# Fillers for TensorE's waits, GpSimd copies of V, and more PSUM banks for the u transposes, in the first two batches of a fused attention and mixer kernel

## The chip, the cores and the metric

The kernel runs on one core of one Trainium2 chip. The metric is the device time in microseconds of one execution. A core has TensorE (PE in the profile; PEld is its weight load), VectorE (DVE), ScalarE (ACT), GpSimd (POOL) and SyncE (SP, which here only issues DMAs). Matmul results go to PSUM, which has eight banks of 2 KB per partition; the other engines run their own instruction streams in order and wait for each other by semaphores.

## The reference

Eight batches of sliding-window causal attention (8 heads, 576 positions, head size 64, window 64), followed by a mixer: a low-rank mix over positions and a two-layer MLP over the 512 channels, each with a residual.

```python
scores = scale * np.matmul(q, k.transpose(0, 1, 3, 2))
scores = np.where((rel >= 0) & (rel < 64), scores, -1e9)      # rel = query pos - key pos
attn = softmax(scores); o = np.matmul(attn, v)
x = o.transpose(0, 2, 1, 3).reshape(B, S, H * D)              # 8 x 576 x 512
h = x.transpose(0, 2, 1) @ U @ V                              # U 576x32, V 32x576
u = x + h.transpose(0, 2, 1)
ch = np.maximum(u @ w_ch1, 0.0) @ w_ch2                       # 512 -> 2048 -> 512
return u + ch
```

## The kernel before

All 4608 tokens (8 x 576) are cut into 36 tiles of 128 and nine chunks of 512. The work of a batch comes in pieces:

- T: `TK(j)` and `TQ(j)` transpose K and Q of a pair of heads on PE (line 245: for the first four batches twelve small transposes). ACT copies the K result into `kt` (line 263), DVE the Q result into `qt` (line 268).
- S: `SC(j)` computes the scores of a pair of heads (line 275), ACT takes the exponential into `pts` (line 290), DVE multiplies with the 0/1 `maskA` (line 291). `SC8` does the last block of all heads.
- PV: `PV(t)` multiplies with V for one tile of 128 positions (line 321); DVE takes reciprocals of the sums and scales into `x` (lines 330, 331). V is held twice: `vA` as it is loaded, and `vB` shifted by 64 positions. The shift is made by `shift_v` (lines 135 and 136 in two large copies, lines 140 and 141 in seven copies of 64 x 512).
- U and V: five matmuls with `ub` (U in bf16, cast from `uf`), an ACT copy into `hh`, then the matmuls with `vrep` (the mixer's V, four times below each other) on line 360. Batches 0 and 1 (`alone`) add x by a matmul with the identity (line 368), and DVE and ACT copy the sums into the tiles `un` (line 383).
- UT: `UT(t)` transposes a tile of u on PE (line 398) and copies it into `uTc`, the input of the MLP (line 402).

The MLP of a chunk, `mlp(c)`, has 16 pieces `ch1` (four matmuls each, `psA`, line 424, then ReLU into `c1`) and 16 pieces `ch2` (four matmuls each, `psU`, line 446; after every fourth, DVE adds u and SP issues the output). The order is written out by hand. Batch 0's attention runs first and alone. Then, for chunk c, the pieces of batch c+1 (and T of batch c+2 from batch 3 on) are put behind the MLP's 32 pieces by tables of slots: `PLACE_1` for batch 1, `PLACE_2` for batch 2, `PLACE` for the rest. Slot 32 is behind the last MLP piece. Each engine runs its instructions in the order in which they are written.

PSUM: `ps_mm` has three banks (MLP results, and three of four transpose groups of batch 0), `ps_big` two buffers of two banks (scores, PV, U, V), `ps_tp` one bank (the other transposes). Batch 0's `shift_v` is done by ACT, between the scores and PV:

```python
a["S"][HP]()
for _ in load_kq(2, False):
    pass
shift_v(0, nc.scalar.copy, range(NFULL))
for f in a["PV"]:
    f()
```

Most loads are issued by POOL and cast to bf16 on the way: K and Q of batch 0, its V, `vrep`, the halves of `w1b` and `w2b`, then K, Q and V of batch 1, in this order. POOL also makes the identity and `maskA` (lines 163 to 181).

Of the kernel before, what the change touches and what calls it, by code (L numbers as in the profile page):

```python
# [12 lines left out]
BF16 = mybir.dt.bfloat16  # L13
FP32 = mybir.dt.float32
# [3 lines left out]
def kernel(  # L18
# [39 lines left out]
    const = ctx.enter_context(tc.tile_pool(name="const", bufs=1))  # L58
# [6 lines left out]
    ps_mm = ctx.enter_context(tc.tile_pool(name="ps_mm", bufs=3, space=bass.MemoryType.PSUM))  # L65
    ps_big = ctx.enter_context(tc.tile_pool(name="ps_big", bufs=2, space=bass.MemoryType.PSUM))
    ps_tp = ctx.enter_context(tc.tile_pool(name="ps_tp", bufs=1, space=bass.MemoryType.PSUM))

    ctx.enter_context(tc.manual_schedule())

# [6 lines left out]
    uf = [const.tile([P, NT, R], FP32, name=f"uf{i}") for i in range(2)]  # L77
    ub = [const.tile([P, NT, R], BF16, name=f"ub{i}") for i in range(2)]
    vrep = const.tile([P, W + S + W], BF16, name="vrep")
    xs = [const.tile([P, NT, H, D], BF16, name=f"xs{i}") for i in range(2)]  # L80
    vA = [const.tile([P, NFULL, H, VW], BF16, name=f"vA{i}") for i in range(2)]
    vB = [const.tile([P, NFULL, H, VW], BF16, name=f"vB{i}") for i in range(2)]
# [49 lines left out]
    def shift_v(b, copy, tiles=None):  # L132
        va, vb = vA[b % 2], vB[b % 2]
        if tiles is None:
            copy(out=vb[0:W, :, :, 0:D], in_=va[W:P, :, :, 0:D])
            copy(out=vb[W:P, 0 : NFULL - 1, :, 0:D], in_=va[0:W, 1:NFULL, :, 0:D])
            return
        for t in tiles:
            if t > 0:
                copy(out=vb[W:P, t - 1, :, 0:D], in_=va[0:W, t, :, 0:D])  # L140
            copy(out=vb[0:W, t, :, 0:D], in_=va[W:P, t, :, 0:D])
# [59 lines left out]
        out=uf[1][:, 1:NT, :], in_=moe_U[W:S, :].rearrange("(c p) r -> p c r", p=P)  # L201
    )
    for g in range(4):
        nc.gpsimd.dma_start(out=vrep[g * R : (g + 1) * R, W : W + S], in_=moe_V[:, :])
    w1v = moe_w_ch1.rearrange("(c p) n -> p c n", p=P)
    for lo, hi in ((0, 1024), (1024, 2048)):
        nc.gpsimd.dma_start(out=w1b[:, :, lo:hi], in_=w1v[:, :, lo:hi])
    w2v = moe_w_ch2.rearrange("(i p) m -> p i m", p=P)
    for lo, hi in ((0, 8), (8, 16)):
        nc.gpsimd.dma_start(out=w2b[:, lo:hi, :], in_=w2v[:, lo:hi, :])  # L210
# [7 lines left out]
    def uT_of(c):  # L218
        if c not in uT_tiles:
            uT_tiles[c] = uT_pool.tile([P, NDC, CH], BF16, name="uTc")  # L220
        return uT_tiles[c]


    def attention(b, spare=False, alone=False):
# [9 lines left out]

        def tr(src, j):
            if grouped:
                if spare and turn[0] % 4 != 0:
                    tpb = ps_mm.tile([P, 2 * CH], BF16, name="tpm", tag="mm")
                    tp = tpb[:, 0:S].rearrange("d (c p) -> d c p", c=GR)
                else:  # L240
                    tp = ps_tp.tile([P, GR, GP], BF16, name="tpg", tag="tp")
                turn[0] += 1
                for c in range(GR):
                    for g in range(2):
                        nc.tensor.transpose(  # L245
                            tp[g * D : (g + 1) * D, c, :], src[:, 2 * j + g, c, :], ident[0:GP, 0:GP]
                        )
# [145 lines left out]
        def UT(t):  # L393
            def f():
                g = g0 + t
                tp = ps_tp.tile([P, NDC, P], BF16, name="tpu", tag="tp")
                for dc in range(NDC):
                    nc.tensor.transpose(  # L398
                        tp[:, dc, :], u_tiles[g][:, dc * P : (dc + 1) * P], ident[:]
                    )  # L400
                col = (g % TPC) * P
                nc.scalar.copy(out=uT_of(g // TPC)[:, :, col : col + P], in_=tp[:])  # L402
            return f

        pcs["T"] = [f for j in range(HP) for f in (TK(j), TQ(j))]
# [10 lines left out]
    def mlp(c):  # L416
        uTc = uT_of(c)
        c1 = [None] * NFC

        def ch1(i):  # L420
            def f():
                ps = ps_mm.tile([P, CH], FP32, name="psA", tag="mm")
                for dc in range(NDC):
                    nc.tensor.matmul(  # L424
                        ps[:],
                        w1b[:, dc, i * P : (i + 1) * P],
                        uTc[:, dc, :],
                        start=(dc == 0),
                        stop=(dc == NDC - 1),
                    )  # L430
                c1[i] = c1_pool.tile([P, CH], BF16, name=f"c1_{i}")
                if i in DVE_RELU:
                    nc.vector.tensor_relu(out=c1[i][:], in_=ps[:])
                else:
                    nc.scalar.activation(out=c1[i][:], in_=ps[:], func=ACT.Relu)
            return f

        acc = {}

        def ch2(t, quarter):  # L440
            def f():
                g = c * TPC + t
                if quarter == 0:
                    acc[t] = ps_mm.tile([P, DM], FP32, name="psU", tag="mm")
                for i in range(4 * quarter, 4 * quarter + 4):
                    nc.tensor.matmul(  # L446
                        acc[t][:],
                        c1[i][:, t * P : (t + 1) * P],
                        w2b[:, i, :],
                        start=(i == 0),  # L450
                        stop=(i == NFC - 1),
                    )
# [17 lines left out]
        "UT": [24, 25, 26, 27, 28],  # L470
    }
    PLACE_1 = {
        "T": [22, 23, 24, 25, 26, 27, 28, 28],
        "S": [24, 26, 28, 29, 29],
        "PV": [30, 31, 32, 32, 32],
        "U": [32],
        "V": [32, 32, 32],
        "UT": [32, 32, 32, 32, 32],
# [3 lines left out]
    PLACE_2["S"] = [3, 5, 7, 9, 10]  # L482


    att = {0: attention(0, spare=True, alone=True)}
    a = att[0]
    for j in range(HP):
        a["T"][2 * j]()
        a["T"][2 * j + 1]()
        if j > 0:  # L490
            a["S"][j - 1]()
    a["S"][HP - 1]()
    a["S"][HP]()
    for _ in load_kq(2, False):
        pass
    shift_v(0, nc.scalar.copy, range(NFULL))
    for f in a["PV"]:
        f()
    for i in range(2):
        nc.vector.tensor_copy(out=ub[i][:], in_=uf[i][:])  # L500
    for part in ("U", "V", "UT"):
        for f in a[part]:
            f()
    load_v(2)


    for c in range(NCH):
        slots = [[] for _ in range(NSLOT + 1)]

        def place(b, parts, where):  # L510
            if b not in att:
                att[b] = attention(b, alone=(b == 1))
            for part in parts:
                for f, s in zip(att[b][part], where[part]):
                    slots[s].append(f)

# [51 lines left out]
```

## Time and profile before

| | |
|---|---|
| median of 3 runs | 378.45 us (378.31 to 379.71) |
| the profiled execution | 379.35 us, its span 377.3 us |
| PE busy | 343.0 us, 91% of the span |
| DVE, ACT, POOL busy | 177.5, 131.1, 108.6 us |
| granted TensorE clock, mean | 0.973 |
| 0 to 30 us: PE busy | 16.4 us |
| 65 to 95 us: PE busy | 20.6 us |

The span is from the first to the last instruction of the profiled execution. The granted clock is the share of TensorE's full clock that the chip allowed, 1.00 being full speed; a row of a busy-time view gives it for its stretch. In a row of the instructions in order of time stand the start and the duration in us, the engine and the kernel's line, the operation with what it writes and reads, and in brackets how long the engine had been idle before it and what released it. The end of a matmul is modelled, so the pace of a stream of matmuls is read from the distance of their starts.

### The profile page before, as it was taken

The numbers are of one execution on the slowest core, as the hardware profiler recorded it, in microseconds if no ns is written. First come the engines' busy times: TensorE is split into PE (matmuls) and PEld (weight loads), VectorE is DVE, ScalarE is ACT, GpSimd is POOL, SyncE is SP. The second block draws the span as 40 slices with busy tenths as digits, with TensorE's granted clock in tenths as the row PEclk, the third lists the DMA queues.
The fourth block names the chain that finished last, engine by engine and source line by source line (L and its number), as shares of the span: only waits on it lengthen the run. The fifth ranks groups of instructions, "written<-read, shape, count | busy, mean of one in ns | idle before, by whom it ended". The sixth has DMA issues, their size and how long they took to land.

```text
span 377.3 us, 7086 instructions
## 1 busy us (share of the span) xinstructions
PE 343.0 (91%) x3030; PEld 170.1 (45%) x3082; DVE 177.5 (47%) x313; ACT 131.1 (35%) x200; POOL 108.6 (29%) x125
## 2 busy tenths in 40 slices
PE   3566999666999999999999999999999999999996
PEld 2433444323544544554455445544554445444442
DVE  4551323550665636554655465546455653322421
ACT  2734213314552345234523452344235403300300
POOL 8761184088008700484038304300000000000000
PEclk9997999886999999999999999999999999999999
DMA  7999999299009910999099809100010002002002
GB/s 95 139 209 200 190 171 197 55 112 105 3 2 118 129 57 0 92 99 112 2 93 108 102 3 90 57 30 0 30 57 28 2 30 84 0 30 83 0 30 84
DMA packets 91135, 28.54 MB, mean 76 GB/s; under 512 B 77152, under 2 KB 85472, under 8 KB 91104
## 3 DMA queue, kind: packets, MB, share of 16 engines
q0 software_dynamic: 84704, 18.50, 56.6%
q1 hardware_dynamic: 6400, 9.59, 7.4%
q8 instruction: 24, 0.39, 0.4%
q14 instruction: 7, 0.06, 0.0%
HBM read 37.14 MB, written 9.44 MB: 123 GB/s over the span
## 4 chain that ended last, share of the span: by engine, by line
PE 84%; DVE 5%; ACT 5%; issue 2%; POOL 2%; DMA 1%; ACTq 0%; DVEq 0%; POOLq 0%
PE psA L424 35%; PE psU L446 31%; PE xr L321 3%; PE tpn L251 3%; PE psv L360 3%; PE sc L275 3%; PE tpu L398 3%; PE tpg L245 2%; ACT pts L290 1%; PE pshh L345 1%; ACT uTc L402 1%; DMA qg<-in_q_dram 1%; DVE xs_97 L331 1%; DVE osb L455 1%; PE psv L368 1%
## 5 line engine op out<-in xcount | busy, mean ns | idle before, releaser
L424 PE MATMUL psA<-uTc,w1b 128*128 128x512 bf16 x556 | 135.0, 388 | 2.0 <-ACT uTc L402 0.7
L424 PEld LDWEIGHTS <-w1b 128*128 128x128 bf16 x576 | 53.9, 99 | 63.3 <-issue 5.2
L455 DVE TENSOR_TENSOR osb<-psU,un 128x512 f32<-128x512 f32 x36 | 24.8, 690 | 59.5 <-PE psU L446 56.5
L291 DVE TENSOR_TENSOR pts<-pts,maskA 128x1024 bf16<-128x1024 bf16 x32 | 23.0, 719 | 36.3 <-ACT pts L290 36.3
L290 ACT ACTIVATE pts<-sc 128x1024 bf16<-128x1024 f32 x32 | 32.7, 1022 | 14.7 <-PE sc L275 14.7
L402 ACT COPY uTc<-tpu 128x512 bf16<-128x512 bf16 x36 | 21.1, 586 | 32.3 <-PE tpu L398 32.3
L123 POOL DMA_DIRECT2D vA_99<-in_v_dram x16 | 14.1, 884 | 54.7 <-PE xr L321 47.4
L123 POOL DMA_DIRECT2D vA_98<-in_v_dram x16 | 14.1, 883 | 38.9 <-PE xr L321 33.5
L321 PEld LDWEIGHTS <-pts 128*64 128x64 bf16 x576 | 14.7, 115 | 18.7 <-issue 11.7
L398 PE MATMUL tpu<-ident,un 128*128 128x128 bf16 x144 | 14.7, 228 | 5.6 <-ACT uTc L402 5.6
L398 PEld LDWEIGHTS <-un 128*128 128x128 bf16 x144 | 11.3, 101 | 13.4 <-issue 6.5
L360 PE MATMUL psv<-hh,vrep 128*128 128x512 bf16 x38 | 14.6, 428 | 2.0 <-ACT hh L353 1.3
L245 PE MATMUL tpg<-ident,kg 96*64 96x96 bf16 x168 | 7.0, 224 | 8.0 <-DMA kg<-in_k_dram 5.2
L331 DVE TENSOR_TENSOR xs_97<-xr,rcp 128x512 bf16<-128x512 f32 (+1 forms) x20 | 13.8, 692 | 0.7
L331 DVE TENSOR_TENSOR xs_96<-xr,rcp 128x512 bf16<-128x512 f32 (+1 forms) x20 | 13.8, 690 | 0.7
L245 PEld LDWEIGHTS <-kg 96*64 96x64 bf16 x192 | 6.6, 125 | 13.8 <-issue 6.7
L330 DVE RECIPROCAL rcp<-xr 128x8 f32<-128x8 f32 (+1 forms) x40 | 8.2, 204 | 9.7 <-PE xr L321 9.6
L385 DVE TENSOR_TENSOR un<-psv,xs_97 128x512 bf16<-128x512 f32 (+1 forms) x15 | 9.8, 687 | 5.2 <-PE psv L360 5.2
L385 DVE TENSOR_TENSOR un<-psv,xs_96 128x512 bf16<-128x512 f32 (+1 forms) x15 | 9.5, 683 | 3.4 <-PE psv L360 3.4
L353 ACT CAST hh<-pshh 128x512 bf16<-128x512 f32 x8 | 4.7, 589 | 16.7 <-PE pshh L345 16.7
L321 PE MATMUL xr<-vA_99,pts 128*64 128x65 bf16 x160 | 8.9, 197 | 1.6 <-DVE xs_97 L331 1.4
L114 POOL DMA_DIRECT2D kn_103<-in_k_dram x10 | 8.7, 872 | 4.9 <-PE tpn L251 4.9
(571 smaller groups left out, 609.6 us busy)
## 6 DMA issues: line engine op xcount, KB each, us to landing
out_dram<-osb SPq DMA_DIRECT2D x36, 256.0 KB, 2.0
vA_98<-in_v_dram POOLq DMA_DIRECT2D x16, 128.0 KB, 5.1
w1b<-in_moe_w_ch_dram POOLq DMA_DIRECT2D x2, 1024.0 KB, 10.2
w2b<-in_moe_w_ch_dram POOLq DMA_DIRECT2D x2, 1024.0 KB, 17.7
vA_99<-in_v_dram POOLq DMA_DIRECT2D x16, 128.0 KB, 4.6
kg<-in_k_dram POOLq DMA_DIRECT2D x3, 576.0 KB, 13.1
qg<-in_q_dram POOLq DMA_DIRECT2D x3, 576.0 KB, 14.2
kn_102<-in_k_dram POOLq DMA_DIRECT2D x8, 128.0 KB, 4.4
```

The costliest lines, as they stand in the source:

```text
L123: nc.gpsimd.dma_start(out=va[:, t, :, 0:D], in_=v[b, :, t * P : (t + 1) * P, :].rearrange("h p d -> p h d"),)
L245: nc.tensor.transpose(tp[g * D : (g + 1) * D, c, :], src[:, 2 * j + g, c, :], ident[0:GP, 0:GP])
L290: nc.scalar.activation(out=dst, in_=sc[:], func=ACT.Exp, scale=scale)
L291: nc.vector.tensor_tensor(out=dst, in0=dst, in1=maskA.rearrange("p g n w -> p g (n w)"), op=ALU.mult)
L321: nc.tensor.matmul(xr[r0 : r0 + W, h // 4, (h % 4) * VW : (h % 4 + 1) * VW], pts[:, h // 2, h % 2, blk, :], rhs, start=True, stop=True,)
L331: nc.vector.tensor_tensor(out=x[lo:hi, t, :, :].rearrange("p (a h) d -> p a h d", a=2), in0=xv[:, :, :, 0:D], in1=rcp[lo:hi].to_broadcast( ...
L360: nc.tensor.matmul(ps[:, n, :], vrep[:, off : off + P], hh["sb"][:], start=True, stop=not alone,)
L398: nc.tensor.transpose(tp[:, dc, :], u_tiles[g][:, dc * P : (dc + 1) * P], ident[:])
L402: nc.scalar.copy(out=uT_of(g // TPC)[:, :, col : col + P], in_=tp[:])
L424: nc.tensor.matmul(ps[:], w1b[:, dc, i * P : (i + 1) * P], uTc[:, dc, :], start=(dc == 0), stop=(dc == NDC - 1),)
L446: nc.tensor.matmul(acc[t][:], c1[i][:, t * P : (t + 1) * P], w2b[:, i, :], start=(i == 0), stop=(i == NFC - 1),)
L455: nc.vector.tensor_tensor(out=osb[:], in0=acc[t][:], in1=u_tiles[g][:], op=ALU.add)
```

## The change

Five things are changed, all in what runs before and during the MLP of the first chunk:

1. Batch 0's `shift_v` is done by POOL, behind the issues of `w1b` and ahead of those of `w2b`.
2. `vrep` is no longer loaded with a cast by POOL. SP loads it in float32 into the new tile `vf`, and DVE casts it, behind the first mask of batch 0; the casts of `uf` to `ub` move to the same place from behind PV.
3. In batches 0 and 1, `UT(t)` takes a bank of the `mm` pool for t not divisible by 4, and DVE makes the copy for even t.
4. `turn_over(n)` issues n matmuls of the identity with 256 columns of `maskA` into a bank that nobody reads. It is called behind transposes, PV, U, V and UT of batch 0, and behind the pieces of batch 1 in the last slot, UT excepted.
5. While batch 0 runs, the three `mm` banks are two for `mm` and one for these matmuls (so two of three transpose groups of batch 0 go to `mm`); then the three-bank pool is opened in their place. In batch 1, `more_room` takes one `mm` buffer for them. `PLACE_1` has T and S, and the first three PV, one slot earlier.

```diff
+    first = ExitStack()
+    psum = {
+        "mm": first.enter_context(tc.tile_pool(name="ps_t0", bufs=2, ...)),
+        "spare": first.enter_context(tc.tile_pool(name="ps_s0", bufs=1, ...)),
+    }
...
     for g in range(4):
-        nc.gpsimd.dma_start(out=vrep[g * R : (g + 1) * R, W : W + S], in_=moe_V[:, :])
+        nc.sync.dma_start(out=vf[g * R : (g + 1) * R, :], in_=moe_V[:, :])
     ... # w1b issues
+    shift_v(0, nc.gpsimd.tensor_copy, range(NFULL))
     ... # w2b issues
...
-                if spare and turn[0] % 4 != 0:
-                    tpb = ps_mm.tile([P, 2 * CH], BF16, name="tpm", tag="mm")
+                if spare and turn[0] % 3 != 0:
+                    tpb = psum["mm"].tile([P, 2 * CH], BF16, name="tpm", tag="mm")
...
-                tp = ps_tp.tile([P, NDC, P], BF16, name="tpu", tag="tp")
+                if alone and t % 4 != 0:
+                    tpb = psum["mm"].tile([P, 2 * CH], BF16, name="tpv", tag="mm")
+                    tp = tpb[:, 0 : NDC * P].rearrange("p (c q) -> p c q", q=P)
+                else:
+                    tp = ps_tp.tile([P, NDC, P], BF16, name="tpu", tag="tp")
...
-                nc.scalar.copy(out=uT_of(g // TPC)[:, :, col : col + P], in_=tp[:])
+                copy = nc.vector.tensor_copy if alone and t % 2 == 0 else nc.scalar.copy
+                copy(out=uT_of(g // TPC)[:, :, col : col + P], in_=tp[:])
...
     PLACE_1 = {
-        "T": [22, 23, 24, 25, 26, 27, 28, 28],
-        "S": [24, 26, 28, 29, 29],
-        "PV": [30, 31, 32, 32, 32],
+        "T": [21, 22, 23, 24, 25, 26, 27, 27],
+        "S": [23, 25, 27, 28, 28],
+        "PV": [29, 30, 31, 32, 32],
...
+    spare_bank = [psum["spare"].tile([P, CH], FP32, name="spare")]
+    def turn_over(n):
+        for _ in range(n):
+            nc.tensor.matmul(
+                spare_bank[0][:, 0:256], ident[:],
+                maskA[:, 0, 0:4, :].rearrange("p n w -> p (n w)"),
+                start=True, stop=True,
+            )
+    def more_room():
+        spare_bank[0] = psum["mm"].tile([P, CH], FP32, name="spare", tag="mm")
...
     for j in range(HP):
         a["T"][2 * j]()
+        turn_over(2)
         a["T"][2 * j + 1]()
+        turn_over(2)
         if j > 0:
             a["S"][j - 1]()
+        if j == 1:
+            for i in range(2):
+                nc.vector.tensor_copy(out=ub[i][:], in_=uf[i][:])
+            nc.vector.tensor_copy(out=vrep[:, W : W + S], in_=vf[:])
     a["S"][HP - 1]()
     a["S"][HP]()
     for _ in load_kq(2, False):
         pass
-    shift_v(0, nc.scalar.copy, range(NFULL))
+    turn_over(2)
     for f in a["PV"]:
         f()
-    for i in range(2):
-        nc.vector.tensor_copy(out=ub[i][:], in_=uf[i][:])
-    for part in ("U", "V", "UT"):
+        turn_over(2)
+    a["U"][0]()
+    turn_over(3)
+    for part in ("V", "UT"):
         for f in a[part]:
             f()
+            turn_over(1)
+    first.close()
+    psum["mm"] = ctx.enter_context(tc.tile_pool(name="ps_mm", bufs=3, ...))
     load_v(2)
...
                 for f, s in zip(att[b][part], where[part]):
                     slots[s].append(f)
+                    if s == NSLOT and part != "UT":
+                        slots[s].append(lambda: turn_over(2))
...
+            if b == 1:
+                slots[NSLOT].append(more_room)
             place(b, ("S", "PV"), where)
```

More of the change, by code (lines that the diff above doesn't have):

```diff
@@ L64 @@
     out_pool = ctx.enter_context(tc.tile_pool(name="osb", bufs=4))
-    ps_mm = ctx.enter_context(tc.tile_pool(name="ps_mm", bufs=3, space=bass.MemoryType.PSUM))
     ps_big = ctx.enter_context(tc.tile_pool(name="ps_big", bufs=2, space=bass.MemoryType.PSUM))
     ps_tp = ctx.enter_context(tc.tile_pool(name="ps_tp", bufs=1, space=bass.MemoryType.PSUM))
+    first = ExitStack()
+    psum = {
+        "mm": first.enter_context(tc.tile_pool(name="ps_t0", bufs=2, space=bass.MemoryType.PSUM)),
+        "spare": first.enter_context(tc.tile_pool(name="ps_s0", bufs=1, space=bass.MemoryType.PSUM)),
+    }
     ctx.enter_context(tc.manual_schedule())
@@ L79 @@
     vrep = const.tile([P, W + S + W], BF16, name="vrep")
+    vf = const.tile([P, S], FP32, name="vf")
     xs = [const.tile([P, NT, H, D], BF16, name=f"xs{i}") for i in range(2)]
@@ L421, in f @@
             def f():
-                ps = ps_mm.tile([P, CH], FP32, name="psA", tag="mm")
+                ps = psum["mm"].tile([P, CH], FP32, name="psA", tag="mm")
                 for dc in range(NDC):
@@ L443, in f @@
                 if quarter == 0:
-                    acc[t] = ps_mm.tile([P, DM], FP32, name="psU", tag="mm")
+                    acc[t] = psum["mm"].tile([P, DM], FP32, name="psU", tag="mm")
                 for i in range(4 * quarter, 4 * quarter + 4):
@@ L482 @@
     PLACE_2["S"] = [3, 5, 7, 9, 10]
+    spare_bank = [psum["spare"].tile([P, CH], FP32, name="spare")]
+    def turn_over(n):
+        for _ in range(n):
+            nc.tensor.matmul(
+                spare_bank[0][:, 0:256],
+                ident[:],
+                maskA[:, 0, 0:4, :].rearrange("p n w -> p (n w)"),
+                start=True,
+                stop=True,
+            )
+    def more_room():
+        spare_bank[0] = psum["mm"].tile([P, CH], FP32, name="spare", tag="mm")
     att = {0: attention(0, spare=True, alone=True)}
@@ L495 @@
         pass
-    shift_v(0, nc.scalar.copy, range(NFULL))
+    turn_over(2)
     for f in a["PV"]:
         f()
-    for i in range(2):
-        nc.vector.tensor_copy(out=ub[i][:], in_=uf[i][:])
-    for part in ("U", "V", "UT"):
+        turn_over(2)
+    a["U"][0]()
+    turn_over(3)
+    for part in ("V", "UT"):
         for f in a[part]:
             f()
+            turn_over(1)
+    first.close()
+    psum["mm"] = ctx.enter_context(
+        tc.tile_pool(name="ps_mm", bufs=3, space=bass.MemoryType.PSUM)
+    )
     load_v(2)
```

## The prediction, made before the changed kernel was run

> **What bounds the kernel now.** I read the page first, for the span and the row of the granted clock, then the busy time of each engine in stretches of 3.41 us, then the instructions in order of time around batches 0 and 1, and last the waits of the first 40 us.
>
> ```profile
> span 377.3 us, 7086 instructions
> PEclk9997999886999999999999999999999999999999
> ```
>
> The profiled execution took 379.35 us for this span; the median of the runs shown is 378.45, 0.9 below it. All differences below are taken inside the profiled execution and subtracted from the median. From the tenth digit on the clock row is full: what can be won lies in the first 95 us, where PE waits, and where its clock is low.
>
> ```profile
> 12.22:15.63 3.41, 2.75 (x69) 2.12 (x65) 2.12 (x3) 2.26 (x3) 3.40 (x6) 1.00 2.28 153
> 29.28:32.70 3.42, 1.53 (x15) 0.94 (x14) 1.28 (x2) 1.66 (x3) 0.87 (x1) 1.00 1.22 198
> 32.70:39.52 6.82, 5.47 (x17) 2.19 (x16) 0.69 (x1) 1.77 (x3) 0.69 (x1) 0.50 1.23 201
> 66.83:70.24 3.41, 1.00 (x36) 0.81 (x37) 1.65 (x4) 0.64 (x1) 0.00 (x0) 1.00 0.44 112
> 70.24:73.66 3.42, 3.09 (x45) 1.52 (x39) 1.38 (x2) 1.74 (x2) 0.00 (x0) 0.50 0.00 0
> 73.66:77.07 3.41, 2.88 (x47) 1.41 (x45) 2.94 (x7) 0.80 (x2) 0.18 (x1) 1.00 0.00 0
> 80.48:83.90 3.42, 2.53 (x7) 1.08 (x8) 0.69 (x1) 0.66 (x2) 3.42 (x5) 0.50 2.13 131
> 83.90:87.31 3.41, 1.70 (x13) 0.81 (x11) 1.34 (x2) 2.17 (x4) 3.41 (x5) 1.00 2.44 144
> 87.31:94.14 6.83, 5.45 (x32) 2.59 (x31) 0.00 (x0) 2.99 (x5) 5.58 (x5) 0.50 1.47 93
> ```
>
> The second number is the length, the third PE's busy time, the one after POOL's the granted clock. The clock is halved in exactly these stretches, each one or two times 3.41 us long; their edges lie on one grid (32.70 to 70.24 is 11 x 3.413). A stretch with PE busy for at most 1.70 of 3.41 (29.28, 66.83, 83.90) is followed by half clock; one with 2.88 (73.66) is not. Full matmuls busy for 2.53 (80.48) bring it back, but 2.75 of transposes and scores (12.22) did not:
>
> ```profile
> 26.61 0.63 PE L360 MATMUL psv<-hh,vrep 128*128 128x512 bf16 x1 [0.22 <-issue]
> 27.04 0.63 PE L368 MATMUL psv<-xs_96,ident 128*128 128x512 bf16 x1
> ```
>
> ```profile
> 51.06 0.38 PE L446 MATMUL psU<-w2b,c_1_552 128*128 128x512 bf16 x1
> 51.28 0.38 PE L446 MATMUL psU<-w2b,c_2_559 128*128 128x512 bf16 x1
> ```
>
> At 27 us, where the row still says 1.00, matmuls of 512 columns follow each other at 0.43; at 51 us at 0.22. So PE ran at half speed from the start, before any recorded change, until about 29.3. A filler of 256 columns is half of that: an estimate of 0.21 us cold, 0.11 warm.
>
> **The change, part by part. A: up to the first V matmul of batch 0 (25.81 us).**
>
> ```profile
> 5.93 1.02 POOL L181 TENSOR_SCALAR_AFFINE_SELECT maskA<-maskA 128x896 bf16<-128x896 bf16 x1
> 12.41 0.61 PE L275 MATMUL sc<-qt_111,kt_107 64*128 64x64 bf16 x16
> 12.95 0.69 PE L245 MATMUL tpm<-ident,kg 96*64 96x96 bf16 x12
> 13.65 0.69 PE L245 MATMUL tpm<-ident,qg 96*64 96x96 bf16 x12
> 15.53 0.61 PE L275 MATMUL sc<-qt_113,kt_109 64*128 64x64 bf16 x16 [0.64 <-DVE qt_113 L268]
> 17.57 0.61 ACT L141 COPY vB_100<-vA_98 64x512 bf16<-64x512 bf16 x1
> 21.42 0.62 ACT L141 COPY vB_100<-vA_98 64x512 bf16<-64x512 bf16 x1
> 23.97 0.67 DVE L500 CAST ub_94<-uf_92 128x160 bf16<-128x160 f32 x1
> 25.81 0.59 PE L360 MATMUL psv<-hh,vrep 128*128 128x512 bf16 x1 [0.67 <-ACT hh L353]
> PE xr L321 <- ACT vB_100 L140: 1.8, 3, 0.6
> 52.86 1.89 POOL L135 COPY vB_101<-vA_99 64x2048 bf16<-64x2048 bf16 x1
> 65.13 1.47 POOL L136 COPY vB_100<-vA_98 64x1536 bf16<-64x1536 bf16 x1
> 65.60 1.54 DVE L291 TENSOR_TENSOR pts<-pts,maskA 128x1024 bf16<-128x1024 bf16 x1 [2.19 <-ACT pts L290]
> ```
>
> Gains: ACT's seven copies (17.57 to 22.04) made PE wait 1.8, and the casts of ub (to 24.64) held U by about 0.8 after the last attention result. On POOL a 64x512 copy is 0.63 by the two POOL rows (0.82 ns per element, 0.21 fixed), seven 4.4; they stand behind the two w1b issues, ahead of which the four vrep issues are gone. SP takes those as f32 loads; it has nothing else to do before the first output. The casts, and the new one of vrep, go into a pause of DVE after the first mask.
>
> Costs: a filler reads maskA, which POOL finishes only at 6.95 (5.93 + 1.02). PE is in order, so batch 0's first Q transposes wait there until 6.95, and all K and Q loads behind find PE late; that is also why I cost the earlier V load at nothing: what it delays, PE would not have taken before. From 6.95, cold: eight pairs of fillers at 0.43, seven transpose groups at 0.70 (12.95 to 13.65), three score groups at 0.54 (12.41 to 12.95) come to 9.9, so the fourth score group starts at 16.9 instead of 15.53: 1.35 late. Were PE warm from its second full window on, every one of these takes about half and the group comes at about 15.4, no loss. POOL's copies can also hold up DVE's masks: the row at 65.60 took 1.54 beside a POOL copy that ended at 66.60. The five filler pairs among the PVs come to 2.1 cold, more than the 1.8 that they fill, so cold, that is not won either. A is thus between 0.8 - 1.35, about -0.6, and 0.8 + 1.8 less 0.6 for a mask held up, +2.0. I take +0.5, nearer the cold end, as the row of 12.22 shows transposes and scores failing to lift the clock; by 22 us PV matmuls and fillers without a pause should have done it, so V starts warm.
>
> The Trainium skill, on the page TensorE: Matmul & The Clock Gate, Part 4 (PE-mode transpose), says that a transpose does not count as PE-busy in the same way. By that rule alone A would be -0.6 and the sum 1.1 smaller. The row of 12.22 agrees with it but mixes in scores, so it doesn't prove it.
>
> **B: V to the first MLP matmul of batch 0.**
>
> ```profile
> 6.22 0.76 DVE L268 COPY qt_110<-tpm 128x576 bf16<-128x576 bf16 x1 [1.57 <-PE tpm L245]
> 27.71 0.69 DVE L383 CAST un<-psv 128x512 bf16<-128x512 f32 x1 [3.07 <-PE psv L368]
> 28.44 0.58 ACT L383 CAST un<-psv 128x512 bf16<-128x512 f32 x1 [2.68 <-DVE un L383]
> 31.27 0.38 PE L398 MATMUL tpu<-ident,un 128*128 128x128 bf16 x4 [1.22 <-ACT uTc L402]
> 31.69 0.58 ACT L402 COPY uTc<-tpu 128x512 bf16<-128x512 bf16 x1 [0.47 <-PE tpu L398]
> 34.64 7.74 PE L424 MATMUL psA<-uTc,w1b 128*128 128x512 bf16 x24 [0.67 <-ACT uTc L402]
> ```
>
> Before, from 25.81 to 34.64 is 8.83. In it ten V matmuls run cold, and the four transposes of u share one bank: each waits for the ACT copy of the one before. After, counted from the first V matmul and warm: four matmuls end at 0.86, result at 1.03; DVE copy to 1.76, ACT copy behind it to 2.38 (the row of 28.44 shows that it waits for DVE); second four done at 2.0, DVE to 2.74, ACT to 3.36; the last two wait for the buffer, done at 3.04, DVE to 3.75. Then the u transposes, 0.2 each, in three banks: DVE copies the first to 4.48 and the third to 5.2 (0.68 each, 512/576 of 0.76), ACT the second to 4.3 and, its bank being that of the second, the fourth to 5.36. MLP starts at 5.4: 3.4 won. Bounds: 0.9, if all of it stays cold (my count then gives 7.9), and 4.2, if two of the copies are not behind each other. I take 3.4. Seven single fillers lie in these waits; uncovered they cost 0.75.
>
> **C: the MLP's first matmuls.** From 34.64 to 39.52 they ran at 0.43; warm they take half: 2.4 won. If the clock falls again in the transposes, one window of 3.41 at half costs 1.7, so the lower bound is 0.7. I take 2.4.
>
> **D: batch 1.**
>
> ```profile
> 68.45 0.45 PE L245 MATMUL tpg<-ident,kg 96*64 96x96 bf16 x12 [1.89 <-DVE qt_112 L268]
> 81.19 0.59 PE L360 MATMUL psv<-hh,vrep 128*128 128x512 bf16 x1 [0.67 <-ACT hh L353]
> 90.23 1.91 PE L424 MATMUL psA<-uTc,w1b 128*128 128x512 bf16 x4
> L331 DVE TENSOR_TENSOR xs_97<-xr,rcp 128x512 bf16<-128x512 f32 (+1 forms) x20 | 13.8, 692 | 0.7
> ```
>
> V to MLP takes 9.04 here; the count of B, with filler pairs and a fifth transpose, gives 5.3: 3.7 won. The MLP matmuls from 90.23 to 94.14 ran at half clock with one transpose group among them: 1.7 won. Moving the pieces one slot earlier puts one more PV before the MLP's end; a PV there costs at least DVE's multiply of 0.69 and a small reciprocal, so about 0.8 is won. Of twelve fillers I leave 0.2 uncovered (all uncovered: 1.3). D is 6.0; cold throughout it would be 0.8 + 1.1 = 1.9.
>
> **E: the stalls of batch 1.** PE waited 1.89 for a DVE copy, and the half clock from 70.24 to 73.66 followed, which cost about half of PE's 3.09 there. The wait comes from the mask at 65.60 that ran beside POOL's shift of V. POOL's shifts come when V's loads land, so they stay where they are (one set begins at 52.86, the other ends at 66.60) while PE is 6 to 7 us earlier: both sets then meet masks of batch 1. One stall goes, one of the same kind comes. Bounds: +3.4, if none comes and the clock holds, and -1.5, if both come and the half clock stays. I take +0.8.
>
> **What the earlier MLP could run into.**
>
> ```profile
> 30.09 0.87 POOL L123 DMA_DIRECT2D vA_99<-in_v_dram  x1 [4.32 <-DMA w1b<-in_moe_w_ch_dram]
> 41.03 0.79 POOL L105 DMA_DIRECT2D kg<-in_k_dram  x1 [4.71 <-DMA w2b<-in_moe_w_ch_dram]
> ```
>
> The second half of w1 lands by 30.1 and w2 by 41.0. With MLP from about 30.7 (25.3 + 5.4), w1's second half is wanted at 30.7 + 32 x 0.22, 37.6, and w2 at 44.5: both are there. POOL's copies stand ahead of w2's issue, at most by their own 4.4 us; w1 is in transfer meanwhile, which hides it. Without that cover w2's second half would land at 45.4, and its first matmul, eight later than the first, wants it at 46.2: still nothing.
>
> **Sum.** 0.5 + 3.4 + 2.4 + 6.0 + 0.8 = 13.1. 379.35 - 13.1 = 366.25 for an execution like the profiled one; from the median, 365.4.
>
> **The rivals.**
> 1. The clock falls again while the u transposes wait. For it: the stretch at 83.90, with 1.70 of transposes and V matmuls, was followed by half clock; against: the fillers add some 0.5 to 0.9 to such a stretch, and the transposes stand closer. Price 1.7 in each batch, and A at its cold end: 365.4 + 3.4 + 1.1 = 369.9.
> 2. The u copies, being split over DVE and ACT into one tile, run one behind the other as the copies of 28.44 do. Then MLP starts at 6.55 instead of 5.4 and 5.3: 2.4 in all, 367.8. Against: those two read one PSUM tile, the new ones read different banks.
> 3. The fillers don't lift the clock at all. Then A -0.6, B 0.9, C 0, D 1.9, E 0: 2.2, so 376.2. Against: plain matmuls at 80.48 did lift it.
> 4. Slower: the fillers stand where PE is not waiting, and the clock stays low. 38 in batch 0 and 12 in batch 1 at 0.21 are 10.5; against them stand rival 3's gains with A's loss left out, 2.8: 378.45 + 7.7, about 386. It decides from 2.8 us of uncovered fillers on. For it: from 6.95 on PE has no pause until the scores are done. Against: at 29.28 and 83.90 PE has 1.9 and 1.7 us free in each 3.41.
> 5. All goes well: A +2.0, E +3.4, so 365.4 - 1.5 - 2.6 = 361.3, and with B at its upper bound 360.5.
>
> **How the numbers follow.** The forecast 0.50, rival 1 0.17, rival 2 0.10, rival 3 0.07, rival 4 0.05, rival 5 0.08, and 0.03 for a loss elsewhere that eats all of it to no change. 0.5% is 1.9 us, about what a measurement of this kernel can tell from no change. Faster 0.92, same 0.03, slower 0.05. The range takes in rivals 1, 2 and 5: 360.5 to 370.9, one microsecond above rival 1 for uncovered fillers; outside lie 0.07 + 0.05 + 0.03 and the tails.
>
> **What the changed profile would show.** The clock row full from the sixth digit on. The second transpose group of batch 0 at about 7.4, behind a filler that waited for POOL's maskA. No ACT rows on vB_100, seven POOL rows of about 0.63 between 15 and 21. First V matmul at 25.3, pitch 0.22; MLP at 5.4 behind it. In batch 1 from the first V matmul to MLP 5.3. I am wrong if V's pitch is 0.43 (rival 3), if half clock stands in the first MLP matmuls (1), if the copies into uTc are strictly one after another (2), or if PE waits for w1 or w2.

## The result, and the profile after

The changed kernel takes 367.25 us (365.84 to 367.81) against 378.38 (375.29 to 379.71) for the kernel before: a ratio of 0.971, 95% interval 0.965 to 0.978, 11.1 us faster. The forecast was 365.4, with a range of 360.5 to 370.9. The profiled executions are 365.84 and 379.35, 13.5 apart, with spans of 364.0 and 377.3. The profiled execution of the changed kernel is the fastest of its four; the others took 367.25 to 367.81.

The page of the changed kernel, its rows of the busy time in stretches of 3.41 us (length, PE, PEld, DVE, ACT and POOL busy, granted clock), and rows in order of time:

```profile
span 364.0 us, 7239 instructions
PEclk9969999999999999999999999999999999999999
```

```profile
10.82:14.23 3.41, 3.41 (x61) 2.08 (x60) 1.97 (x6) 1.55 (x2) 3.41 (x5) 1.00 1.71 146
14.23:17.65 3.42, 3.42 (x70) 2.27 (x65) 2.17 (x3) 1.83 (x3) 3.20 (x5) 1.00 2.39 138
17.65:21.06 3.41, 2.09 (x49) 1.32 (x43) 2.60 (x5) 2.15 (x3) 2.77 (x4) 1.00 1.18 202
21.06:24.47 3.41, 3.22 (x51) 1.81 (x46) 3.12 (x7) 0.00 (x0) 3.41 (x5) 0.50 1.12 211
24.47:27.88 3.41, 3.41 (x19) 1.14 (x17) 1.03 (x3) 0.59 (x1) 2.78 (x4) 0.50 1.15 212
```

```profile
7.00 0.59 PE L500 MATMUL spare<-maskA,ident 128*128 128x256 bf16 x2 [1.73 <-POOL maskA L186]
7.52 0.69 PE L251 MATMUL tpm<-ident,qg 96*64 96x96 bf16 x12
17.16 0.61 PE L281 MATMUL sc<-qt_117,kt_113 64*128 64x64 bf16 x16
27.03 0.59 PE L366 MATMUL psv<-hh,vrep 128*128 128x512 bf16 x1
31.10 0.41 DVE L413 COPY uTc<-tpu 128x512 bf16<-128x512 bf16 x1
31.15 0.59 ACT L413 COPY uTc<-tpv 128x512 bf16<-128x512 bf16 x1 [0.37 <-PE tpv L408]
32.84 3.40 PE L435 MATMUL psA<-uTc,w1b 128*128 128x512 bf16 x15 [0.56 <-ACT uTc L413]
73.64 0.38 PE L366 MATMUL psv<-hh,vrep 128*128 128x512 bf16 x1 [0.35 <-ACT hh L359]
78.48 1.02 PE L435 MATMUL psA<-uTc,w1b 128*128 128x512 bf16 x4 [0.33 <-ACT uTc L413]
80.78 0.45 PE L251 MATMUL tpg<-ident,qg 96*64 96x96 bf16 x12
```

Read against the rows of before, in the order of time:

| piece | before | after | won |
|---|---|---|---|
| first V matmul of batch 0 | 25.81 | 27.03 | -1.2 |
| from there to the MLP | 8.83 | 5.81 | 3.0 |
| the MLP's first matmuls, at 0.43 before, at full clock after | | | 2.4 |
| from there to batch 1's first V matmul | | | 3.3 |
| V to MLP, batch 1 | 9.04 | 4.84 | 4.2 |
| the MLP's first matmuls, chunk 1 (until batch 2's second transpose group) | 4.13 | 2.30 | 1.8 |
| the rest of the span | | | -0.2 |

The third row is half of the 4.88 us in which these matmuls ran cold before. The fourth row is what is left of 81.19 - 73.64 = 7.55 after the three above it; the second transpose group of batch 2 stood at 94.36 before and stands at 80.78, 13.6 earlier. The stretches of half clock that began at 33, 70, 80 and 87 us are gone. One of 6.8 us stands at a new place, from 21.06 to 27.88, from the PVs of batch 0 to its first V matmuls.

### The profile page after: what moved, and what is told of

It reads as the page before. It is cut to its first block, busy times and chain, and to the rows that moved or that the text cites. A ratio compares the mean times of both kernels' runs of the same rounds, so it can differ in the third digit from the quotient of the medians.

```text
span 364.0 us, 7239 instructions
## 1 busy us (share of the span) xinstructions
PE 347.0 (95%) x3132; PEld 170.2 (47%) x3132; DVE 180.0 (49%) x319; ACT 123.8 (34%) x188; POOL 111.9 (31%) x128
## 4 chain that ended last, share of the span: by engine, by line
PE 89%; DVE 5%; ACT 3%; POOL 1%; issue 1%; POOLq 0%
PE psA L435 35%; PE psU L457 33%; PE xr L327 4%; PE tpn L257 3%; PE sc L281 3%; PE psv L366 2%; PE tpg L251 2%; PE spare L500 2%; PE tpu L408 2%; PE pshh L351 1%; ACT pts L296 1%; DVE pts L297 1%; PE tpm L251 1%; DVE xs_101 L337 1%; ACT uTc L413 1%
## 5 line engine op out<-in xcount | busy, mean ns | idle before, releaser
L435 PE MATMUL psA<-uTc,w1b 128*128 128x512 bf16 x576 | 132.9, 380 | 0.9 <-ACT uTc L413 0.9
L435 PEld LDWEIGHTS <-w1b 128*128 128x128 bf16 x576 | 53.0, 98 | 61.1 <-issue 1.0
L413 ACT COPY uTc<-tpu 128x512 bf16<-128x512 bf16 x27 | 15.8, 586 | 28.2 <-PE tpu L408 28.2
L500 PE MATMUL spare<-maskA,ident 128*128 128x256 bf16 x50 | 13.1, 346 | 1.7 <-POOL maskA L186 1.7
L366 PE MATMUL psv<-hh,vrep 128*128 128x512 bf16 x40 | 13.4, 385 | 0.8 <-ACT hh L359 0.3
L408 PE MATMUL tpu<-ident,un 128*128 128x128 bf16 x120 | 11.6, 219 | 0.0
```

The costliest lines, as they stand in the source:

```text
L366: nc.tensor.matmul(ps[:, n, :], vrep[:, off : off + P], hh["sb"][:], start=True, stop=not alone,)
L408: nc.tensor.transpose(tp[:, dc, :], u_tiles[g][:, dc * P : (dc + 1) * P], ident[:])
L435: nc.tensor.matmul(ps[:], w1b[:, dc, i * P : (i + 1) * P], uTc[:, dc, :], start=(dc == 0), stop=(dc == NDC - 1),)
L500: nc.tensor.matmul(spare_bank[0][:, 0:256], ident[:], maskA[:, 0, 0:4, :].rearrange("p n w -> p (n w)"), start=True, stop=True,)
```

## Which part made the gain: the experiments

Two theories were set against each other. One: the fillers hold the clock, and the clock is most of the gain. The other: the shorter waits for the u transposes are most of it, and the fillers mostly cost. Nearly all runs are read by their median and their ratio to the kernel before, run beside them.

| kernel | median us | ratio (95%) |
|---|---|---|
| changed kernel | 367.25 | 0.971 (0.965 to 0.978) |
| without fillers | 368.34 | 0.974 (0.969 to 0.978) |
| fillers as transposes | 367.69 | 0.972 (0.967 to 0.978) |
| without T fillers | 364.35 | 0.966 (0.961 to 0.971) |
| u transposes as before | 371.38 | 0.985 (0.979 to 0.991) |
| shift of V on ACT | 367.88 | 0.971 (0.966 to 0.976) |
| fillers with an early operand | 366.72 | 0.969 (0.964 to 0.973) |
| fillers in batch 1 only | 366.62 | 0.966 (0.961 to 0.971) |
| before, with fillers alone | 375.85 | 0.989 (0.984 to 0.995) |
| old slots | 366.78 | 0.971 (0.967 to 0.976) |
| before, with the u transposes alone | 370.09 | 0.979 (0.974 to 0.983) |
| without T fillers, late load of vf | 365.07 | 0.966 (0.961 to 0.970) |
| the same, split V tiles | 363.90 | 0.966 (0.961 to 0.972) |

Single executions of one kernel lie up to 6 us apart. Often the longer ones have the lower mean clock (the kernel before with fillers alone took 373.5 at 0.994 and 379.3 at 0.981), but not always: the fastest execution of the changed kernel, 365.84, has its lowest clock, 0.988 against 0.995 to 0.999. Presumably the grid of 3.41 us falls differently on each; that was not tested. One of the six executions without T fillers took 1893 us, and no run shows why; the other five took 363.94 to 368.17. Each trace is of one execution. A difference of about 1 us between two of these kernels is therefore not told apart by the medians.

**Without fillers.**

```diff
-        for _ in range(n):
+        for _ in range(0):
```

> The changed kernel without any filler matmul; all else as changed. Theory 1 (the clock): V of batch 0 is cold again (ten matmuls at 0.43), so are the first MLP matmuls of chunk 0 (2.4 us) and those of chunk 1 (1.8 us), and the clock falls in batch 1; the T stage of batch 0 gets 1.2 to 1.6 us back. Net 4 to 8 us slower than the changed kernel: 371 to 375 us, granted clock back at about 0.97. Theory 2 (the copies and banks make the gain, fillers only cost): the clock rows stay as in the changed kernel or do not matter, 365 to 367 us.

The edit also leaves batch 1 the MLP's PSUM buffer that the fillers took. The kernel takes 368.34: 1.1 us more, between the theories and outside both, and no more than the medians scatter. Order of time and the stretches of its trace:

```profile
25.54 0.59 PE L366 MATMUL psv<-hh,vrep 128*128 128x512 bf16 x1 [0.67 <-ACT hh L359]
26.35 0.63 PE L366 MATMUL psv<-hh,vrep 128*128 128x512 bf16 x1
26.78 0.63 PE L374 MATMUL psv<-xs,ident 128*128 128x512 bf16 x1
28.82 0.38 PE L366 MATMUL psv<-hh,vrep 128*128 128x512 bf16 x1
31.93 8.36 PE L435 MATMUL psA<-uTc,w1b 128*128 128x512 bf16 x38 [0.67 <-ACT uTc L413]
28.72:32.13 3.41, 2.03 (x20) 1.35 (x19) 1.94 (x4) 1.70 (x4) 0.88 (x1) 1.00 1.24 207
73.10:79.93 6.83, 6.15 (x24) 2.91 (x24) 2.41 (x4) 2.01 (x4) 6.83 (x9) 0.50 2.42 133
```

V is cold (0.43 apart), yet the MLP starts at 31.93, 0.9 earlier than with fillers, 6.39 behind the first V matmul, and runs at full clock: by 28.82 V's own matmuls are back at it. After that a half clock stands only in batch 1, 6.8 us long; V to MLP takes 6.59 there (74.37 to 80.96), against 4.84 with fillers.

**The u transposes alone, on the kernel before.**

```diff
+                if alone and t % 4 != 0:
+                    tpb = ps_mm.tile([P, 2 * CH], BF16, name="tpv", tag="mm")
...
+                copy = nc.vector.tensor_copy if alone and t % 2 == 0 else nc.scalar.copy
```

> The kernel before with the u transposes of batches 0 and 1 alone changed: three banks, copies split over DVE and ACT; no fillers, nothing else. Theory 1 (only the waits shrink): from V to MLP about 6.5 to 7 us instead of 8.8 and 9.0, so 4 to 5 us faster than before, 373.5 to 374.5 us, with the first MLP matmuls still at half clock. Theory 2 (with the waits shorter the clock follows without fillers): first MLP matmuls at full clock as well, 2 to 4 us more, 370 to 372 us.

370.09 against 377.62: 7.5 us, the second theory, from a few lines that add no matmul. In order of time:

```profile
26.28 0.59 PE L360 MATMUL psv<-hh,vrep 128*128 128x512 bf16 x1 [0.67 <-ACT hh L353]
29.17 0.38 PE L368 MATMUL psv<-xs,ident 128*128 128x512 bf16 x1
29.98 0.38 PE L402 MATMUL tpu<-ident,un 128*128 128x128 bf16 x4
32.03 8.14 PE L429 MATMUL psA<-uTc,w1b 128*128 128x512 bf16 x36 [0.67 <-ACT uTc L407]
74.77 0.59 PE L360 MATMUL psv<-hh,vrep 128*128 128x512 bf16 x1 [0.67 <-ACT hh L353]
81.36 1.02 PE L429 MATMUL psA<-uTc,w1b 128*128 128x512 bf16 x4 [0.45 <-ACT uTc L407]
82.69 1.04 PE L429 MATMUL psA<-uTc,w1b 128*128 128x512 bf16 x4
```

```profile
73.25:80.08 6.83, 5.68 (x21) 2.66 (x22) 2.44 (x5) 1.76 (x3) 6.83 (x9) 0.52 2.32 135
```

In batch 0, V to MLP is 5.75 with no filler, as short as in the changed kernel. From the first u transpose to the MLP it is 2.0 us, and both chunks' MLPs start at full clock (four matmuls in 1.02, 1.91 before). V itself has not got its clock back: batch 0's is cold up to 28.8, and batch 1's runs at half clock (the last fence), as in the run without fillers, so that V to MLP takes 6.59 there (74.77 to 81.36). In every trace with these banks and the fillers of batch 1 it is 4.59 to 5.71.

**The u transposes as before, all else changed.**

```diff
-                if alone and t % 4 != 0:
+                if False:
...
-                copy = nc.vector.tensor_copy if alone and t % 2 == 0 else nc.scalar.copy
+                copy = nc.scalar.copy
```

> The u transposes of batches 0 and 1 go back to one bank with all copies on ACT; fillers and all else as changed. If the banks and the split copies carry their part: from the first V matmul to MLP about 7.7 to 8 us instead of 5.8 in batch 0, and about 7 instead of 4.8 in batch 1, so 4 us slower than the changed kernel, 371 us; the clock may fall once more. If the clock alone carries the V to MLP gain: within 1 us, 367 to 368 us.

371.38, as the first theory of this run said, though in its trace V to MLP takes 7.19 in batch 0 and 8.94, not 7, in batch 1. The busy time in stretches:

```profile
30.91:34.32 3.41, 1.48 (x15) 0.99 (x15) 0.10 (x1) 1.99 (x4) 0.14 (x1) 1.00 1.24 205
34.32:37.74 3.42, 3.27 (x8) 1.17 (x8) 0.00 (x0) 0.69 (x2) 0.55 (x1) 0.53 1.24 205
```

With one bank, a single filler per transpose leaves PE busy for 1.48 of 3.41, and the MLP's first matmuls run at half clock: in this execution the fillers did not hold the clock where the waits stayed. It is the slowest of four (375.39 at a mean clock of 0.985; the others took 370.00 to 372.14 at 0.995 to 0.998), so how often that happens isn't shown.

**Fillers alone, on the kernel before.** The edit adds `turn_over` and the PSUM that it takes from the MLP's pool (one of three banks in batch 0, one buffer in batch 1), and nothing else.

> The kernel before with the fillers and their PSUM bank alone: shift of V on ACT, vrep cast by POOL's loads, u transposes in one bank with ACT copies, old slots. Theory 1 (fillers are worth about 1 us, as leaving them out of the changed kernel showed): 376.5 to 378 us. Theory 2 (the kernel before has more cold stretches than the changed one without fillers, so they are worth 4 to 6 us here): 372 to 374 us. If they cost more than they bring where nothing else is shortened: 379 to 381 us.

375.85, 2.6 us faster by the medians and 1.1% (4 us) by the ratio: between the two theories. In its trace the fillers do hold the clock behind the one-bank u transposes of batch 0 (the MLP starts at full clock, 14 matmuls in 3.18 from 37.08), but not in batch 1, where half clock stands from 80.2 to 83.6 and from 90.4 to 93.8.

**No fillers among batch 0's transposes, and an operand that is ready early.**

```diff
         a["T"][2 * j]()
-        turn_over(2)
         a["T"][2 * j + 1]()
-        turn_over(2)
```

> Only the 16 fillers among the transposes of batch 0 are left out. Theory 1a (they cost in the T stage and do not lift the clock in time): the fourth score group is at 15.5 to 16 instead of 17.2, the first V matmul 1 to 1.6 us earlier, 365.5 to 366.5 us. Theory 1b (they are what makes PV and V warm): V of batch 0 starts cold and stays cold longer, at most 2 us more than in the changed kernel, so 367 to 368.5 us.

364.35, faster than theory 1a asked for. The second run keeps all fillers, but they read a tile that DVE sets at the start (`early[:]` in place of `maskA`):

> The fillers read a small tile that DVE sets first of all, in place of maskA. Theory 1 (the T fillers' cost is the wait for POOL's maskA until 7.0): the second transpose group goes back to about 5.6, the fourth score group from 17.2 to 16 to 16.6, 365.5 to 366.5 us. Theory 2 (the cost is their PE time between cold transposes): the fourth score group stays within 0.4 us of 17.2, 367 to 367.7 us. Without any T filler it stood at 15.4 and the time was 364.35.

366.72, between the two; the trace tells them apart. In order of time, the first fence without T fillers, the second with the early operand:

```profile
5.54 0.69 PE L251 MATMUL tpm<-ident,qg 96*64 96x96 bf16 x12 [0.26 <-DMA qg<-in_q_dram]
15.40 0.61 PE L281 MATMUL sc<-qt,kt 64*128 64x64 bf16 x16 [0.32 <-DVE qt L274]
25.07 0.38 PE L366 MATMUL psv<-hh,vrep 128*128 128x512 bf16 x1 [0.24 <-ACT hh L359]
30.48 9.87 PE L435 MATMUL psA<-uTc,w1b 128*128 128x512 bf16 x45 [0.56 <-ACT uTc L413]
```

```profile
5.78 0.69 PE L253 MATMUL tpm<-ident,qg 96*64 96x96 bf16 x12
15.46 1.03 PE L283 MATMUL sc<-qt,kt 64*128 64x64 bf16 x32
25.70 0.81 PE L368 MATMUL psv<-hh,vrep 128*128 128x512 bf16 x2 [0.24 <-ACT hh L361]
```

The first V matmul is at 27.03 in the changed kernel, 25.70 with the early operand, 25.07 without T fillers. So of the 2.0 us that these fillers cost there, about 1.3 are the wait for maskA until 7.0 and 0.6 their time between cold transposes. The wait itself stands in the changed kernel's row at 7.00; the split is an estimate from single traces (in two kernels whose batch 0 is the same, without any filler in it, this matmul is at 25.54 and at 24.35). The total shows less of it: with the early operand it is only 0.5 below the changed kernel, within the scatter. V is at full clock without the T fillers too (the 0.38 at 25.07).

The two runs without fillers, of all kinds and of the T kind, also price the rest: the 34 other fillers bring 4.0 us (368.34 without any, 364.35 with them; 366.27 to 368.39 against four of six executions at 363.94 to 364.57), and the 16 T fillers cost 2.9 (367.25 against 364.35).

**Fillers in batch 1 only** (all 38 of batch 0 left out).

> All 38 fillers of batch 0 left out, the 12 of batch 1 kept. Theory 1 (fillers pay only where the clock fell without them, in batch 1's V): the half clock from 73 to 79.5 that stands without any filler goes, 3 us: 365 to 365.6 us. Theory 2 (those in batch 0's PV, U, V and UT pay as well, by keeping V and the first MLP matmuls warm): between this kernel and the one without T fillers (364.35) lie 1 to 3 us, this one 366 to 367.5 us.

366.62, the second theory's figure, but its executions run from 363.3 to 368.8, so which of batch 0's fillers pay isn't settled; the medians rank this kernel 2.3 behind the one without T fillers alone. In its trace V to MLP is 4.84 in batch 1, as with all fillers, and 6.40 in batch 0, where V is cold, against 5.41 without the T fillers alone.

**Fillers as transposes.**

```diff
-            nc.tensor.matmul(spare_bank[0][:, 0:256], ident[:], maskA[...], ...)
+            for i in range(2):
+                nc.tensor.transpose(spare_bank[0][:, i * P : (i + 1) * P], maskA[...], ident[:])
```

> Each filler of 256 columns becomes two PE transposes of 128 columns into the same unread bank: the same time on PE, but transposes. If transposes count for the clock as matmuls do: as the changed kernel, 366 to 369 us, first V matmuls of batch 0 at full speed by the same window. If they do not count (the row 12.22 of before, 2.75 us of transposes and scores without effect): the clock as without fillers, and the fillers' time is paid as well, 373 to 377 us.

367.69: like the matmuls. In its trace PE had only PVs and these transposes between 20.55 and 23.96:

```profile
20.55:23.96 3.41, 3.41 (x64) 2.62 (x63) 2.95 (x7) 0.00 (x0) 3.29 (x6) 1.00 1.12 213
22.74 0.61 PE L501 MATMUL spare<-ident,maskA 128*128 128x128 bf16 x4
24.60 0.40 PE L501 MATMUL spare<-ident,maskA 128*128 128x128 bf16 x4
```

Four of them take 0.61 before the end of that stretch and 0.40 after it, so the clock came up. The Trainium skill's sentence that a transpose does not count as PE-busy in the same way (TensorE: Matmul & The Clock Gate, Part 4) finds no support here; as PVs stood among them, it is not disproved. Nor do the times of warming decide it: with matmuls as fillers the kernel with the old slots came to full speed only at 26.4, the changed kernel at 17.65.

**The shift of V back on ACT.** `shift_v(0, nc.scalar.copy, range(NFULL))` in its old place.

> The changed kernel with batch 0's shift of V back on ACT, ahead of the fillers and PV as in the kernel before; all else as changed. Theory 1 (POOL's copies free PV, worth up to the 1.8 us that PE waited): PV waits for ACT's seven copies again, first V matmul 1 to 2 us later, 368.5 to 369.5 us. Theory 2 (on POOL they cost what they save: DVE's masks of scores 2, 3 and 8 were held up by 0.2, 0.3 and 0.4 us beside POOL copies, and cold PVs with fillers are paced at 1.12 us anyway): within 0.7 us, 366.5 to 368 us.

367.88, the second theory. In order of time, first the changed kernel, then this one:

```profile
18.43 1.71 DVE L297 TENSOR_TENSOR pts<-pts,maskA 128x1024 bf16<-128x1024 bf16 x2 [1.32 <-ACT pts L296]
20.06 0.82 DVE L310 TENSOR_TENSOR pts<-pts,maskA 128x512 bf16<-128x512 bf16 x1
```

```profile
19.37 0.69 DVE L296 TENSOR_TENSOR pts<-pts,maskA 128x1024 bf16<-128x1024 bf16 x1 [0.23 <-ACT pts L295]
19.98 0.42 DVE L309 TENSOR_TENSOR pts<-pts,maskA 128x512 bf16<-128x512 bf16 x1
27.13 0.81 PE L365 MATMUL psv<-hh,vrep 128*128 128x512 bf16 x2 [0.24 <-ACT hh L358]
```

Beside POOL's copies the masks take longer (0.82 instead of 0.42), and the first V matmul comes at 27.03 and at 27.13: the move to POOL is worth nothing that can be measured in this kernel.

From there on the two kernels are the same code, yet batch 1 went differently. First the changed kernel, then this one:

```profile
63.87 1.47 POOL L141 COPY vB_104<-vA_102 64x1536 bf16<-64x1536 bf16 x1
64.67 2.00 DVE L297 TENSOR_TENSOR pts<-pts,maskA 128x1024 bf16<-128x1024 bf16 x2 [0.65 <-ACT pts L296]
66.72 0.25 PE L327 MATMUL xr<-vA_103,pts 128*64 128x65 bf16 x2 [0.38 <-DVE pts L297]
```

```profile
64.37 3.14 DVE L296 TENSOR_TENSOR pts<-pts,maskA 128x1024 bf16<-128x1024 bf16 x2 [0.64 <-ACT pts L295]
65.16 1.81 POOL L141 COPY vB<-vA 64x1536 bf16<-64x1536 bf16 x1
67.56 0.25 PE L326 MATMUL xr<-vA,pts 128*64 128x65 bf16 x2 [1.52 <-DVE pts L296]
```

POOL's shift of V ended at 65.34 in the one and at 66.97 in the other, where both masks ran beside it. There PE waited 1.52, and half clock stood from 68.8 to 72.3. Batch 1's first V matmul came 40.80 behind the MLP's start in the changed kernel and 42.92 here; in the traces with transposes as fillers and with the early operand, the same code in batch 1 but for the fillers, 43.62 and 43.61. The profiled execution of the changed kernel escaped this stall.

**The old slots.** `PLACE_1` as before.

> The changed kernel with batch 1's old slots (transposes, scores and PV one slot later). Theory 1 (one more PV behind the last MLP piece, paced by DVE at 0.85): 0.8 us slower than the changed kernel, 368 us. Theory 2 (the slot moves the transposes out of the way of nothing, and the clock's windows decide): within 0.5 us of 367.25.

366.78: the second theory; the moved slots bring nothing that can be measured.

**The late load of vf**, on the kernel without T fillers. DVE clears a column of `vf` behind the second mask, so that SP's loads wait for it, and ACT casts.

> The changed kernel without T fillers, and with the float32 load of the mixer's V held on SP until DVE has done the second score mask, cast by ACT behind the last exponential. Theory 1 (the early load delays batch 0's K and Q: the third K transpose waited until 10.5 to 11.9 without T fillers, 9.9 in the kernel before): that group back at 9.9 to 10.2, the fourth score group at 15.0 or earlier, 363.3 to 364.1 us against 364.35. Theory 2 (the load is hidden): within 0.3 us, and if the later load meets the wide loads it may cost up to 0.5.

365.07, ratio 0.966 as without it. The first theory's gain did not come: the third K transpose is at 10.16 (10.53 without), but the fourth score group at 15.46 (15.40). By the median it is 0.7 slower, a little more than the second theory allowed and within the scatter. **Split V tiles**, on top of that:

```diff
+                    if alone and n:
+                        one = psum["mm"].tile([P, CH], FP32, name="psw", tag="mm")
+                        pst = one[:]
```

> The kernel of the late load, and in batches 0 and 1 every second V result in a PSUM tile of its own from the MLP's pool, so that DVE's and ACT's copies of u need not read one tile. Theory 1 (the ACT copies stood behind DVE's because they share a PSUM tile): the two copies of a pair start within 0.5 us of each other, V to MLP 0.5 to 0.8 shorter in each batch, 1 to 1.6 us faster than the kernel of the late load. Theory 2 (the transposes' copies are the last wait anyway): within 0.4 us of it.

363.90, the lowest median of all, though its interval is that of the kernel without T fillers: four executions took 363.8 to 363.9, two 367.6 and 367.9. The ACT copy no longer waits for DVE's:

```profile
26.22 0.69 DVE L393 CAST un<-psv 128x512 bf16<-128x512 f32 x1 [1.73 <-PE pshh L349]
26.65 0.59 ACT L393 CAST un<-psw 128x512 bf16<-128x512 f32 x1 [1.11 <-PE psw L378]
30.52 9.66 PE L439 MATMUL psA<-uTc,w1b 128*128 128x512 bf16 x43 [0.56 <-ACT uTc L417]
```

V to MLP in batch 0 is 4.93 (25.59 to 30.52), 0.5 less than in the kernel of the late load; 1.2 by the medians is within what they scatter.

## Why the prediction came out right, step by step

The total was right, 13.1 forecast for a pair like the profiled ones and 13.5 measured, 11.1 by the medians. Its steps were not all right, and that the total agrees is in part luck: A came out 1.7 below its forecast, the slots and E 1.9 above theirs, in an execution that escaped a stall.

- **A, +0.5 forecast, -1.2 measured.** This step failed, below its own cold end of -0.6. The wait for maskA at 7.0 was foreseen, and the fourth score group came at 17.16 (16.9 forecast cold; a pair of fillers took 0.54, from 13.32 to 13.86, not 0.43). From there to the first V matmul only 0.4 was won (10.28 before, 9.87 after), where even the cold end counted 0.8 for the casts; that end also left out the 0.3 by which its cold filler pairs (2.1) exceed the wait that they fill (1.8). What failed too is that PVs and fillers would have lifted the clock by 22 us: PE was busy for 3.41 of 3.41 from 10.82 on, the clock came up only at 17.65 and fell again at 21.06, behind a stretch in which PE had been busy for 2.09, waiting for exponentials and masks. The PVs' fillers then ran at half clock in a stretch of 3.22 busy without effect. The clock is not the main loss, though: with the old slots, whose batch 0 is the same code, PE stayed cold up to 26.4, and the first V matmul came at 27.20. The 1.8 us that PE waited for ACT's copies were not won either, as the run with ACT showed.
- **B, 3.4 forecast, 3.0 measured**, although V's first two matmuls were still cold. In six traces with these banks and V warm (without T fillers, with the shift on ACT and others) the length is 5.40 or 5.41, the 5.4 of the count. One place in the count was too long: DVE copies a transposed tile in 0.41, not the 0.68 that I scaled from the Q copy. That copy writes its tile with a stride; whether this is the reason wasn't tested. The price of cold V matmuls was put too high: the count went from 5.4 to 7.9 with everything cold, but without fillers, with eight of V's ten matmuls cold, the length is 6.39, 1.0 more than warm.
- **C, 2.4 and 2.4**, but the fillers aren't needed for it: it comes with the u transposes alone. In the trace with the fillers alone it comes too.
- **D, 3.7 + 1.7 forecast, 4.2 + 1.8 measured.** Of the 4.2, about 2.4 come from the u transposes (9.04 to 6.59 in the trace without fillers) and 1.8 from the clock that batch 1's fillers kept (6.59 to 4.84).
- **The slots and E, 0.8 - 0.2 + 0.8 = 1.4 forecast, 3.3 measured.** The half clock at 70 us, worth half of 3.09, did not come; nor did the stall of 1.89. That was this execution's luck: with the shift on ACT a stall of 1.52 and the half clock came, and batch 1's V was 2.1 later behind the MLP's start, which would leave 1.2 of the 3.3. The slot itself gave nothing.
- **The rivals.** The copies into uTc do overlap (31.10 and 31.15), so rival 2 did not happen. Rival 1's fall of the clock in the u transposes did not happen in the changed kernel's trace; in that with one bank, it did. Rival 3 was half true: fillers alone bring 2.6 by the medians. The T fillers are rival 4's mechanism, at 2.0 us up to V and 2.9 in the total instead of 10.

What the forecast missed as a whole is how the two effects hang together. It counted waits and clock as separate terms; in fact the short waits gave the MLP its clock back by themselves, while V stayed cold without fillers, for the most part in batch 0 and throughout in batch 1. So the gains overlap: the u transposes bring 7.5 alone, and taking them out of the changed kernel costs 4.1. The fillers' net share is 1 us in the changed kernel, no more than the scatter, because the T fillers eat 2.9 of the 4.0 that the others bring; on the kernel before it is some 3 to 4. The earlier casts of `ub` were not tried alone: in the trace with the u transposes alone, U still waited 1.81 for them.

## What to carry to other kernels

Where TensorE's clock falls because it waits, shorten the wait first: three banks and two copying engines, which were not tried one without the other, brought 7.5 us alone, and the MLP's clock came back without a filler. Filler matmuls paid here where PE still waited (34 of them 4.0 us) and cost where PE had no pause to fill or their operand was late (the 16 among batch 0's transposes 2.9): they must read something that is ready, or they become the wait. Moving a copy off a busy engine was worth nothing here, with cold matmuls and masks held up beside POOL's copies as the next limit. And a price read from one execution, as E was, needs a second one: the same code of batch 1 met this stall in some traces and not in others.

## What was unexpected about the hardware

- A stretch with PE busy throughout does not always lift the clock: 3.41 of 3.41 at 10.82 and 3.22 at 21.06, both of transposes, scores or PVs with fillers among them, did not; 3.42 at 14.23, of transposes, scores and fillers as well (a pair of fillers then took 0.39 at 18.67, 0.61 before), and one with U, fillers and V (24.47) did. With the old slots the same code of batch 0 stayed cold up to 26.4. Nor does the busy time alone say when the clock falls: 2.09 at 17.65 was followed by half clock, 2.03 at 28.72 without fillers was not. The edges ahead of the first recorded change are the grid drawn backwards. What the chip counts is not the busy time of the profile, and these runs don't show what it is.
- The granted clock's row says 1.00 until its first recorded change, while matmuls run at half speed (0.43 apart at 26 us without fillers). The distance of the starts is the better witness.
- DVE copies 128x512 bf16 from PSUM in 0.41 where ACT takes 0.59; from float32 they took 0.69 and 0.59.
